# Weight quarters in two loads each, wider zero products, and another fixed order of the opening

## The chip, the cores and the metric

The kernel runs on one core of a Trainium2 chip. The metric is device time in microseconds (us): 188.25 us for the kernel before, the median of 4 runs from 188.14 to 188.42.

A core has five engines that run side by side: TensorE multiplies matrices (PE in the profile; its weight loads are PEld), VectorE (DVE), ScalarE (ACT) and GpSimd (POOL) work on tiles, and SyncE (SP) issues the transfers between the device memory and the core's own memory. Sixteen transfer engines carry these out.

## The reference

First a linear attention with decay, for 4 batches, 8 heads, 768 positions and a head width of 48. Then a feed-forward part on the 3072 rows of width 384 that come out.

```python
for t in range(S):
    cur = np.einsum('bhd,bhe->bhde', u[None] * kt, vt)
    y[:, :, t] = np.einsum('bhd,bhde->bhe', rt, state + cur)
    state = wt[:, :, :, None] * state + np.einsum('bhd,bhe->bhde', kt, vt)
...
x = np.ascontiguousarray(attn_out.transpose(0, 2, 1, 3)).reshape(B * S, H * D)
h = x @ w_in                      # 384 x 2048
g = np.maximum(0.01 * h, h)
out = (g @ w_out)                 # 2048 x 384
```

## The kernel before

**Tiles and stages.** The 3072 rows are 24 chunks of 128, six to a batch. Chunks 0 and 1, and 2 and 3, are handled as pairs (one load for both), the others singly. For a chunk, four loads bring w, k, r and v (lines 493). ScalarE takes the logarithm of w (tile lw, line 360), TensorE sums it along the positions (tiles cp, hp, op; lines 544, 554, 714), ScalarE takes exponentials (line 370), and products of these with r and k (tile rk, line 300) are transposed on TensorE (line 418; for chunks 12 and on by a transposing transfer, line 408) into rkT. Scores (lines 652, 764) are masked on VectorE (tile m, line 436), and with the state (s, sb) they give y (lines 669, 677, 794, 799; its last sum is line 467). y is transposed into xT (lines 481, 295, or by a transfer, line 473). The vector u is brought by a small load on ScalarE's queue and spread over the partitions by a product on TensorE (line 504).

**The feed-forward part.** Each of the two weight matrices is loaded in four quarters (lines 319 and 324), each as one transfer into a staging tile of the ring `in`, and cast to bf16 by two half casts on whichever engine the order says (lines 295, 297). For each chunk TensorE makes four groups of 12 products with w_in, one for each quarter (tile hp, line 837; "up"), ScalarE applies the activation (tile g, line 879), and four groups of 4 products with w_out (tile op, line 898; "down") give the output, which is copied and stored.

**What sets the order.** Every step is entered into a `Plan` with its engine, an assumed duration, its dependencies and a priority. `Plan.order` plays the steps forward in time, engine by engine, and the kernel emits the instructions in the order of the planned starts. The order of each engine is thereby fixed when the program is built. Steps named in the string `EARLY` (numbers count the steps in the order in which the code adds them; a letter picks the engine) get the highest priorities in the order of the string. The list `FIRST` gives the order in which the up and down groups of chunks 0 to 3 are entered. From chunk 4 on, ups of a chunk alternate with downs of the one before.

**Fillers.** Up to a planned time of 24 us (`WARM`), whenever the plan has TensorE waiting before a step, products with a tile of zeros are emitted (line 933); their result is not used.

```python
for _ in range(int((plan.start[i] - at) * 0.7 / 0.13)):
    nc.tensor.matmul(
        op_r.tiles[1][:, 0:256], lhsT=zeros[:, 0:128], rhs=zeros[:], start=True, stop=True)
at = plan.start[i] + plan.dur[i]
```

**The queue of loads.** SP issues the loads in this order: the first pair's w, k, r, v; the second's v, w, k, r; quarters 1 and 0 of w_in, quarter 0 of w_out, quarters 2 and 3 of w_in, quarters 1, 2 and 3 of w_out; then chunk 4's w and r, chunk 5's w, chunk 4's k and v, and so on.

Of the kernel before, what the change touches and what calls it, by code (L numbers as in the profile page):

```python
# [9 lines left out]
BF16 = mybir.dt.bfloat16  # L10
# [5 lines left out]
class Plan:  # L16
# [23 lines left out]
    def order(self):  # L40
        n = len(self.eng)
        users = [[] for _ in range(n)]
        left = [len(d) for d in self.deps]
        for i, d in enumerate(self.deps):
            for j in d:
                users[j].append(i)
        ready_at = [0.0] * n
        start, done = [None] * n, [0.0] * n
        free = {e: 0.8 for e in self.ENGINES}
        coming = {e: [] for e in self.ENGINES}  # L50
        ready = {e: [] for e in self.ENGINES}
        dma_free = 0.0
        flying = []
        for i in range(n):
            if not left[i]:
                heapq.heappush(coming[self.eng[i]], (0.0, i))
        events = [(0.8, e) for e in self.ENGINES]
        heapq.heapify(events)
        count = 0
        while events:  # L60
            now, e = heapq.heappop(events)
            if free[e] > now + 1e-9:
                continue
            while coming[e] and coming[e][0][0] <= now + 1e-9:
                _, i = heapq.heappop(coming[e])
                heapq.heappush(ready[e], (self.pri[i], i))
            if not ready[e]:
                if coming[e]:
                    heapq.heappush(events, (coming[e][0][0], e))
                continue  # L70
            _, i = heapq.heappop(ready[e])
            start[i] = now
            count += 1
            free[e] = now + self.dur[i] * (1.8 if e == "PE" and now < 6 else 1)
            if self.wire[i] is None:
                done[i] = free[e] + self.LAT[e]
            else:

                flying = [x for x in flying if x[0] > free[e]]
                while sum(x[1] for x in flying) + self.rows[i] > 3300:  # L80
                    free[e] = max(free[e], flying.pop(0)[0])
                dma_free = max(dma_free, free[e]) + self.wire[i]
                done[i] = dma_free + 1.7
                flying.append((done[i], self.rows[i]))
            heapq.heappush(events, (free[e], e))
            for j in users[i]:
                left[j] -= 1
                same = self.eng[j] == e and self.wire[i] is None
                ready_at[j] = max(ready_at[j], free[e] if same else done[i])
                if not left[j]:  # L90
                    f = self.eng[j]
                    heapq.heappush(coming[f], (ready_at[j], j))
                    heapq.heappush(events, (max(ready_at[j], free[f]), f))
        assert count == n, (count, n)
        self.start, self.done = start, done
        return sorted(range(n), key=lambda i: (start[i], i))
# [30 lines left out]
def kernel(  # L127
# [11 lines left out]
    nc = tc.nc  # L139
# [14 lines left out]
    AHEAD = 5  # L154

    PAIRS = (0, 2)
    PWIRE, WIRE = 1.53, 1.15
    WEIGHTS = [(4, 24.0)] * 8
    WARM = 24.0
    CASTS = 21  # L160

    EARLY = """
        0 4 1 2 3 5 8 61 7 6 12 58 11 16 13 14 15 21 32 59 17 23 24 18 20p 19 22 28 9a 60 29 30 10a 33
        25 26 31v 40 27 117 64 34 65a 51 36 41a 44 52 63 114 46 42 126 62 45 35 67 66 120 43 71 123 37
        53 47 129 68 132 48 69 135 72 38 75p 49 70 76 74 77p 78 50 81 79 73 87v 54 82 39 118a 85 80 96v
        83 119p 138 86 55 84a 91 115 116 56 95 88v 57 713 128p 715 89 714 97 717 716 127p 98v 719 718 99
        140 122p 729 90v 720 100 121 730 102 723 124a 125p 101 721 724 92v 103 722 727 93 130a 170 104
        94 725 728 131v 105 107 726 106v 731 108 133a 737 109 733 738 134v 110 734 747 136 137p 139 745
        111 748 141 735 142 112 746 144 154v 261 732 113 736 145 172 174 752 147 749 159 149p 155v 171
        146 739 753 148 742 750 200 156 158 152 143a 157v 150 160 755 229 153 151 176 743 162 161 177  # L170
        186 231 756 763 165 265 764 164 230 191 178 758 187v 740 765 232 179 163 759 751 181p 180 202
        233 166 188 766 204 167 190 182 173 245 184 767 206 168 185v 183a 754 192 169v 768 193 741 207
        769 246 194 209 201 771 208 234v 757 770 247 216 262 772 760 210
    """
    blocks = [1] * NCH

    FIRST = [(0,(0,1),(0,1,2,3)),(1,(0,1),(0,1)),(0,(2,),(0,)),(1,(0,1),(2,)),(0,(2,),(1,)),(1,(0,1),(3,)),(0,(2,),(2,3)),(0,(3,),(0,)),(1,(2,),(0,)),(0,(3,),(1,)),(1,(2,),(1,)),(0,(3,),(2,)),(1,(2,),(2,)),(0,(3,),(3,)),(1,(2,),(3,)),(1,(3,),(0,1,2,3))]
    assert sum(blocks) == NCH

    pool = ctx.enter_context(tc.tile_pool(name="pool", bufs=1))  # L180
# [8 lines left out]
    pmask = pool.tile([128, 2, 128], BF16, name="pmask")  # L189
    pev = pool.tile([128, 128], BF16, name="pev")  # L190
    pex = pool.tile([128, 128], BF16, name="pex")
    zeros = pool.tile([128, 256], BF16, name="zeros")
    halves = pool.tile([128, 2], BF16, name="halves")
    ident = pool.tile([128, 128], BF16, name="ident")
    ones = pool.tile([128, 1], BF16, name="ones")
# [34 lines left out]
    with tc.manual_schedule():  # L230
# [80 lines left out]
        win_s, wout_s = [], []  # L311
        JQ = NJ // NQ

        def weight_steps(q, which, pri):
            st = in_r.take()

            def load(st=st, q=q):
                if which == 0:
                    nc.sync.dma_start(
                        out=st.t[:].rearrange("p (t f) -> p t f", t=KT),  # L320
                        in_=w_in_v[:, :, q * 512 : (q + 1) * 512],
                    )
                else:
                    nc.sync.dma_start(
                        out=st.t[:].rearrange("p (t f) -> p t f", t=JQ),
                        in_=w_out_v[:, q * JQ : (q + 1) * JQ, :],
                    )

            ld = step("SP", 0.45, load, pri, writes=[st], wire=2.25, rows=(384, 512)[which])
            made = []  # L330
            for half in range(2):
                def cast(e, st=st, q=q, half=half):
                    if which == 0:
                        f0 = half * 256
                        o = w_in_b[:, :, q * 512 + f0 : q * 512 + f0 + 256]
                        i = st.t[:].rearrange("p (t f) -> p t f", t=KT)[:, :, f0 : f0 + 256]
                    else:
                        n = JQ // 2
                        o = w_out_b[:, q * JQ + half * n : q * JQ + (half + 1) * n, :]
                        i = st.t[:].rearrange("p (t f) -> p t f", t=JQ)[:, half * n : (half + 1) * n, :]  # L340
                    copy(e, o, i)

                made.append(step(
                    ("DVE", "ACT")[half], (0.8, 0.84)[half], cast, CASTS, reads=[st], deps=[ld],
                    DVE=0.8, ACT=0.84, POOL=1.2))
            (win_s if which == 0 else wout_s).append(made)

# [148 lines left out]
        def spread_u():  # L496
            u_row = step(
                "ACT", 0.5,
                lambda: nc.scalar.dma_start(out=ur[:], in_=u.rearrange("h d -> (h d)").unsqueeze(0)),
                -1, wire=0.05)  # L500
            up = pre_r.take()
            s_ub = step(
                "PE", 0.7,
                lambda: nc.tensor.matmul(up.t[:, 0:DM], lhsT=onef[:], rhs=ur[:], start=True, stop=True),
                -1, writes=[up], deps=[u_row])
            return step(
                "ACT", 0.5, lambda: nc.scalar.copy(out=ub[:], in_=up.t[:, 0:DM]), 0.05, reads=[up], deps=[s_ub])
# [411 lines left out]
        for n in range(NCH):  # L919
            if n >= LEAD:  # L920
                plan.deps[lns[n]].append(up_done[n - LEAD])
        for rank, word in enumerate(EARLY.split()):
            i = int(word.rstrip("avp"))
            plan.pri[i] = rank - 10000
            if word[-1] in "avp":
                plan.eng[i] = {"a": "ACT", "v": "DVE", "p": "POOL"}[word[-1]]
                plan.dur[i] = plan.alts[i][plan.eng[i]]

        at = 0.8
        for i in plan.order():  # L930
            if plan.eng[i] == "PE" and at < WARM:
                for _ in range(int((plan.start[i] - at) * 0.7 / 0.13)):
                    nc.tensor.matmul(  # L933
                        op_r.tiles[1][:, 0:256], lhsT=zeros[:, 0:128], rhs=zeros[:], start=True, stop=True)
                at = plan.start[i] + plan.dur[i]
            if plan.alts[i]:
                plan.fn[i](plan.eng[i])
            else:
# [31 lines left out]
```

## Time and profile before

| | |
|---|---|
| median of 4 runs | 188.25 us (188.14 to 188.42) |
| profiled execution | 188.15 us |
| its span, first to last instruction | 186.4 us |
| TensorE busy | 179.5 us, 2608 products |
| VectorE, ScalarE, GpSimd busy | 121.2, 115.9, 101.0 us |
| zero products | 60, 11.7 us of records |
| moved | 34.62 MB, mean 186 GB/s |

The profile is one execution. In a line of its timeline stand the start (us from the span's start), the duration, the engine, the line of the kernel, the operation, the tiles (out<-in), the shape and the count of instructions merged into it; square brackets give idle time before it and what ended it. Records of products overlap, since they are pipelined: from one to the next, the start counts. In the chain of waits a piece is a start, a duration and what the time went to; "issue" is time for which the profile shows no wait. Engines that are not the bottleneck may be idle at no cost.

### The profile page before, as it was taken

How to read it: one execution, taken by the hardware profiler on the slowest of the kernel's cores; microseconds unless marked ns; L12 is line 12 of the kernel's file. 1: busy time of each engine (PE TensorE's matmuls, PEld its weight loads, DVE VectorE, ACT ScalarE, POOL GpSimd, SP SyncE). 2: the span in 40 equal slices, each digit the busy share in tenths (PEclk: the TensorE clock that was granted, in tenths of full speed). 3: DMA queues.
4: the chain of work that ended last, by engine and by line, in shares of the span. 5: the costliest groups of instructions: out<-in, count | busy, mean ns of one | idle time of the engine just before them, and what ended most of it. 6: DMA issues, size and time to landing. Idle time of an engine off the chain costs nothing.

```text
span 186.4 us, 6316 instructions
## 1 busy us (share of the span) xinstructions
PE 179.5 (96%) x2608; PEld 140.5 (75%) x2608; DVE 121.2 (65%) x232; ACT 115.9 (62%) x254; POOL 101.0 (54%) x142
## 2 busy tenths in 40 slices
PE   7999998999999999999999999999999999999892
PEld 4576887877777788787878687778878778788671
DVE  2079994657777797887668786587556676725111
ACT  2395868488665887788677578645465554543330
POOL 7587961133975888878784474351784444620000
PEclk9999999999999999999999999999999999999999
DMA  6999999799498998797999797967999999481202
GB/s 148 261 262 371 387 373 309 151 183 209 121 236 180 210 195 180 167 196 170 176 213 177 169 195 142 219 134 164 219 137 221 173 211 148 102 125 42 67 0 84
DMA packets 116383, 34.62 MB, mean 186 GB/s; under 512 B 109697, under 2 KB 114818, under 8 KB 116354
## 3 DMA queue, kind: packets, MB, share of 16 engines
q1 hardware_dynamic: 116352, 34.22, 85.7%
q8 instruction: 20, 0.33, 0.7%
q14 instruction: 9, 0.07, 0.1%
q10 hardware_dynamic: 2, 0.00, 0.0%
HBM read 25.17 MB, written 4.72 MB: 160 GB/s over the span
## 4 chain that ended last, share of the span: by engine, by line
PE 89%; DVE 3%; DMA 2%; issue 2%; ACT 1%; POOL 1%
PE hp L837 34%; PE op L898 32%; PE op L933 3%; PE se L764 3%; DMA xT<-y 2%; PE yp L799 2%; PE cp L714 2%; PE yp L775 2%; PE yp L794 1%; PE so L418 1%; DVE m L436 1%; PE se L418 1%; POOL rk L300 1%; PE yp L481 1%; PE yp L677 1%
## 5 line engine op out<-in xcount | busy, mean ns | idle before, releaser
L879 ACT ACTIVATE g<-hp 128x512 bf16<-128x512 f32 x96 | 57.2, 597 | 41.0 <-PE hp L837 39.3
L837 PE MATMUL hp<-xT,w_in_b 128*128 128x128 bf16 x1152 | 78.0, 219 | 0.7 <-DMA xT<-y 0.7
L898 PE MATMUL op<-w_out_b,g 128*128 128x384 bf16 x384 | 75.2, 326 | 0.0
L837 PEld LDWEIGHTS <-w_in_b 128*128 128x128 bf16 x1152 | 68.5, 98 | 7.2 <-DMA xT<-y 1.1
L898 PEld LDWEIGHTS <-g 128*128 128x128 bf16 x384 | 33.5, 98 | 15.8
L300 POOL TENSOR_TENSOR sb<-s,a 128x384 bf16<-128x384 f32 x17 | 14.3, 843 | 29.2 <-DVE s L456 14.1
L300 POOL TENSOR_TENSOR ru<-in,ub 128x384 f32<-128x384 f32 x22 | 23.0, 1044 | 7.7 <-DMA in<-in_r_dram 7.7
L300 POOL TENSOR_TENSOR vs<-in,dg 128x384 f32<-128x384 f32 x22 | 18.9, 858 | 9.1 <-DVE dg L393 8.9
L436 DVE TENSOR_TENSOR m<-se,maskb 128x512 bf16<-128x512 f32 x20 | 13.7, 687 | 11.2 <-PE so L764 8.0
L300 POOL TENSOR_TENSOR ru<-ru,in 128x384 f32<-128x384 f32 x20 | 20.4, 1018 | 0.9
L467 DVE TENSOR_TENSOR y<-yp,vs 128x384 bf16<-128x384 f32 x24 | 13.3, 554 | 9.6 <-PE yp L799 6.6
L300 DVE TENSOR_TENSOR rk<-in,ek 128x384 bf16<-128x384 f32 x18 | 14.4, 798 | 3.7 <-ACT ek L370 3.7
L370 ACT ACTIVATE cp<-cp 128x384 f32<-128x384 f32 x22 | 10.6, 483 | 6.3 <-DVE ci L729 6.3
L729 DVE TENSOR_TENSOR ci<-cp,lw 128x384 f32<-128x384 f32 x20 | 11.0, 550 | 4.9 <-PE cp L719 3.3
L300 DVE TENSOR_TENSOR rk<-in,cp 128x384 bf16<-128x384 f32 x22 | 12.0, 547 | 3.2 <-ACT cp L370 2.6
L393 DVE TENSOR_REDUCE dg<-ru 128x8 f32<-128x384 f32 x24 | 13.0, 544 | 1.6 <-POOL ru L300 1.5
L360 ACT ACTIVATE lw<-in 128x384 bf16<-128x384 f32 x24 | 12.2, 521 | 2.9 <-DMA in<-in_w_dram 2.5
L436 DVE TENSOR_TENSOR m<-so,maskb 128x512 bf16<-128x512 f32 x20 | 13.6, 679 | 0.0
L297 DVE COPY o<-op 128x384 f32<-128x384 f32 x10 | 5.6, 555 | 11.7 <-PE op L898 11.5
L933 PE MATMUL op<-zeros 128*128 128x256 bf16 x60 | 11.7, 329 | 1.1 <-DVE zeros L268 1.1
L297 POOL CAST vb<-in 128x384 bf16<-128x384 f32 x19 | 10.5, 554 | 0.7 <-DMA in<-in_v_dram 0.7
L370 ACT ACTIVATE ek<-ci 128x384 f32<-128x384 f32 x20 | 10.4, 519 | 0.8 <-POOL ru L300 0.7
(117 smaller groups left out, 213.5 us busy)
## 6 DMA issues: line engine op xcount, KB each, us to landing
out_dram<-o SPq DMA_DIRECT2D x24, 192.0 KB, 3.0
in<-in_w_dram SPq DMA_DIRECT2D x20, 192.0 KB, 4.0
in<-in_r_dram SPq DMA_DIRECT2D x20, 192.0 KB, 3.7
in<-in_k_dram SPq DMA_DIRECT2D x20, 192.0 KB, 3.7
in<-in_v_dram SPq DMA_DIRECT2D x20, 192.0 KB, 3.7
in<-in_moe_w_in_dram SPq DMA_DIRECT2D x4, 768.0 KB, 11.4
in<-in_moe_w_out_dram SPq DMA_DIRECT2D x4, 768.0 KB, 13.1
in<-in_w_dram SPq DMA_DIRECT2D x2, 384.0 KB, 5.0
```

The source lines that it names most:

```text
L297: (nc.vector if e == "DVE" else nc.gpsimd).tensor_copy(out=o, in_=i)
L300: (nc.vector if e == "DVE" else nc.gpsimd).tensor_tensor(out=o, in0=a, in1=b, op=ALU.mult)
L360: lambda: nc.scalar.activation(out=lw.t[:, :, 0:D], in_=wn.t, func=AF.Ln),
L370: "ACT", 0.5, lambda: nc.scalar.activation(out=out.t[:], in_=i, func=AF.Exp, scale=scale),
L393: lambda: nc.vector.tensor_reduce(out=dg.t[:], in_=ru.t[:], axis=AX.X, op=ALU.add),
L436: lambda par=par: nc.vector.tensor_tensor(out=m.t[:, par], in0=gt(sc[par].t), in1=mask.unsqueeze(1).to_broadcast([128, NP, 128]), op=ALU.m ...
L467: lambda: nc.vector.tensor_tensor(out=y.t[:], in0=hd(yp.t[:, 0:DM]), in1=vs.t[:], op=ALU.add),
L729: lambda: nc.vector.tensor_tensor(out=ci.t[:], in0=hd(cp.t[:, 0:DM]), in1=lw.t[:, :, 0:D], op=ALU.add),
L837: nc.tensor.matmul(hp.t[:, a * N : (a + 1) * N], lhsT=w_in_b[:, t, (j + a) * 128 : (j + a + 1) * 128], rhs=xT[:, t, c0 : c0 + N], start=(a ...
L879: lambda hp=hp, g=g, j=j, J=J, N=N: nc.scalar.activation(out=g.t[:, j : j + J, 0:N], in_=hp.t[:, 0 : J * N].rearrange("p (a n) -> p a n", ...
L898: nc.tensor.matmul(op.t[:, 0:DM], lhsT=g.t[:, j, off : off + 128], rhs=w_out_b[:, j, :], start=(j == 0), stop=(j == NJ - 1))
L933: nc.tensor.matmul(op_r.tiles[1][:, 0:256], lhsT=zeros[:, 0:128], rhs=zeros[:], start=True, stop=True)
```

## The change

- Each weight quarter is loaded by two transfers instead of one, each of half the bytes, into halves of the same staging tile. A half of w_in has runs of 1024 bytes (2048 before), a half of w_out has runs of 768 bytes (1536 before). Each half cast waits for its own load. For w_out the halves are now split along the columns.
- The zero products are 512 columns wide, with at most one of 256 behind them, and their number follows from the planned wait divided by 0.44; the planner assumes TensorE to be slow until 8 us (6 before), and the u load and its product are entered as longer.
- Steps of `EARLY` on one engine now also depend on one another in the order of the string; the string is new and longer (383 steps, 272 before), and so is `FIRST`.

In the new order SP issues the first pair's w, r, k, v; the second's k and w; the second half of quarter 1 of w_in; the second pair's v and r; both halves of quarter 0, the other half of quarter 1, quarters 2 and 3; then w_out's quarters 1 and 0 (as 1, 0, 0, 1), chunk 4's w, w_out's quarters 2 and 3, and chunk 4's r, k, chunk 5's w, chunk 4's v.

TensorE's order around the first groups, before and after (up and down with chunk and quarter, `T` a transpose of rk, `yt` of y, `sc` scores, `st` state):

```
before: ... y1, T3, T3, yt1, st2, up 0.0, up 1.0, up 0.1, up 1.1, down 0.0, sc2, down 1.0, up 1.2, up 0.2,
        y2, up 1.3, up 0.3, yt2, sc3, down 0.1, up 2.1, ...
after:  ... T2, y1, T3, T2, yt1, up 0.0, T3, up 1.0, up 0.1, st2, up 1.1, up 0.2, up 1.2, sc2, up 0.3, up 1.3,
        y2, sc3, down 0.0, yt2, down 1.0, down 1.1, up 2.0, ...
```

```diff
-            free[e] = now + self.dur[i] * (1.8 if e == "PE" and now < 6 else 1)
+            free[e] = now + self.dur[i] * (1.8 if e == "PE" and now < 8 else 1)
...
-    PWIRE, WIRE = 1.53, 1.15
+    PWIRE, WIRE, WWIRE = 1.53, 1.15, (1.12, 1.12)
...
     EARLY = """
-        0 4 1 2 3 5 8 61 7 6 12 58 11 16 13 14 15 21 32 59 17 23 24 18 20p 19 22 28 9a 60 29 30 10a 33
...
+        0 4 2 1 3 5 8 59 7 6 13 58 32 36v 12 17 11 16 22 33 120 14 21 30 15 37 20 24 31 61 23 26 25a 9
...
-    FIRST = [(0,(0,1),(0,1,2,3)),(1,(0,1),(0,1)),(0,(2,),(0,)),(1,(0,1),(2,)),(0,(2,),(1,)),...
+    FIRST = [(0,(0,1),(0,1,2,3)),(0,(2,3),(0,)),(1,(0,1),(0,)),(0,(2,3),(1,)),(1,(0,1),(1,)),...
...
-    zeros = pool.tile([128, 256], BF16, name="zeros")
+    zeros = pool.tile([128, 512], BF16, name="zeros")
...
-            ld = step("SP", 0.45, load, pri, writes=[st], wire=2.25, rows=(384, 512)[which])
...
+                part = st.t[:, half * 768 : (half + 1) * 768].rearrange("p (t f) -> p t f", t=(KT, JQ)[which])
+                if which == 0:
+                    f0 = q * 512 + half * 256
+                    src, dst = w_in_v[:, :, f0 : f0 + 256], w_in_b[:, :, f0 : f0 + 256]
+                else:
+                    n0 = half * DM // 2
+                    src = w_out_v[:, q * JQ : (q + 1) * JQ, n0 : n0 + DM // 2]
+                    dst = w_out_b[:, q * JQ : (q + 1) * JQ, n0 : n0 + DM // 2]
+                ld = step(
+                    "SP", 0.45, lambda part=part, src=src: nc.sync.dma_start(out=part, in_=src), pri,
+                    writes=[st], wire=WWIRE[which], rows=(384, 512)[which])
...
-                -1, wire=0.05)
+                -1, wire=0.75)
...
-                "PE", 0.7,
+                "PE", 1.6 / 1.8,
...
+            if plan.wire[i] is None:
+                plan.deps[i] += behind.get(plan.eng[i], [])
+                behind[plan.eng[i]] = [i]
...
-                for _ in range(int((plan.start[i] - at) * 0.7 / 0.13)):
+                wait = plan.start[i] - at
+                for n in [512] * int(wait / 0.44) + [256] * int(wait % 0.44 / 0.22):
                     nc.tensor.matmul(
-                        op_r.tiles[1][:, 0:256], lhsT=zeros[:, 0:128], rhs=zeros[:], start=True, stop=True)
-                at = plan.start[i] + plan.dur[i]
+                        op_r.tiles[1][:, 0:n], lhsT=zeros[:, 0:128], rhs=zeros[:, 0:n], start=True, stop=True)
+                at = plan.start[i] + plan.dur[i] * (1.8 if plan.start[i] < 8 else 1)
```

## The prediction

> **What bounds the kernel now.** I read the page's part 1 first, then TensorE's timeline of the first 34 us, the chain of waits, the transfer rates by stretch, and the chain's end.
>
> ```profile
> PE 179.5 (96%) x2608; PEld 140.5 (75%) x2608; DVE 121.2 (65%) x232; ACT 115.9 (62%) x254; POOL 101.0 (54%) x142
> ...
> L933 PE MATMUL op<-zeros 128*128 128x256 bf16 x60 | 11.7, 329 | 1.1 <-DVE zeros L268 1.1
> ```
>
> TensorE carries the span, but 60 of its products multiply zeros. All but one lie before the first product of the feed-forward part (w_in, line 837):
>
> ```profile
> 1.12 2.74 PE L933 MATMUL op<-zeros 128*128 128x256 bf16 x12 [1.12 <-DVE zeros L268]
> 3.79 1.64 PE L504 MATMUL op<-ur,onef 1*128 1x384 f32 x2
> 5.37 2.31 PE L933 MATMUL op<-zeros 128*128 128x256 bf16 x10
> 7.48 0.85 PE L544 MATMUL hp<-lw,pev 128*128 128x384 bf16 x2
> ...
> 22.38 1.50 PE L837 MATMUL hp<-xT,w_in_b 128*128 128x128 bf16 x24
> ```
>
> The feed-forward part starts at 22.4. ScalarE's timeline says why: its cast of the needed weight half ran from 21.64 to 22.49. That weight had landed at 20.4 (issue 11.7, 8.7 to landing).
>
> The chain of waits then shows one hole, and after it TensorE is full for 142 us:
>
> ```profile
> 31.04 0.14 PE se L652
> 31.22 0.84 issue
> 32.05 0.21 PE se L652
> 32.28 0.02 PE se L652
> ```
>
> "issue" means that nothing in the profile was waited for. The page's instruction queue moved only 20 packets, 0.33 MB (about 16 KB each). At 31.0 TensorE had just reached a step of 64 tiny instructions (32 products with their weight loads), so I read the hole as late instructions.
>
> The transfers are the other limit of the opening; columns end with clock, transfer share, GB/s:
>
> ```profile
> 6.00:12.00 6.00, 5.78 (x50) 3.92 (x49) 2.39 (x6) 2.90 (x8) 3.46 (x10) 1.00 1.28 261
> 16.00:30.00 14.00, 13.54 (x289) 11.26 (x290) 12.95 (x23) 10.62 (x20) 9.91 (x11) 1.00 1.06 379
> ```
>
> Pair loads (runs of 384 bytes) move at 261 GB/s and land 1.5 us apart, at 4.5, 6.0 ... 15.0. Weight quarters (2048 and 1536 bytes, 786 KB) move at 379 and land 2.05 us apart, at 20.4 to 33.0. The queue never empties.
>
> At the end the last chunk's output is just late:
>
> ```profile
> 171.66 3.93 DMA xT<-y
> 175.60 0.05 issue
> 175.64 1.51 PE hp L837 x24
> ```
>
> TensorE idles 0.72 us here. The profiled execution took 188.15 us: span 186.4 plus 1.75 around it; the median of four is 188.25, 0.10 more. My sum is made against 188.15.
>
> **The change, part by part.**
>
> *Opening fillers.* The planner fills a planned wait with zeros. For the same numbers as the code of before uses (12 and 10 products, as the trace shows), the new rule gives, by hand, 6 wide and 1 narrow before the product for u (planned wait 3.75 - 0.8 = 2.95) and 2 wide before the first sums (wait 1.06). A narrow one takes 2.74/12 = 0.228, so a wide one 0.43 to 0.46 at that clock. The decays (lw) were ready at 4.55 + 0.94 = 5.49, yet the sums started at 7.48, behind ten zeros. Now: u ends near 5.65, two wide fillers end at 6.5. Gain 1.0 us for chunk 0's chain, bounds 0.5 to 1.9. It isn't on the final path by itself, since the weights decide next; without it the next term would lose up to 1 us.
>
> *Half loads and their place.* I counted the steps in the order the code adds them, so that the new order can be read. One half (of quarter 1) goes ahead of the second pair's v and r; then come both halves of quarter 0. One half at 379 GB/s is 393 KB/379 = 1.03 us. Landings: the pair's last load at 15.0 + 1.03 = 16.05. In the trace the first two weights came 5.4 after the last pair load, 1.3 more than their 4.1; I keep the 1.3: quarter 0 at 18.4 and 19.4, then 20.4, 21.5, 22.5, 23.5, 24.6, and the second matrix 25.6, 26.6, 27.7, 28.7.
>
> *The chain to the first product.* Sums at 6.5 take 0.64, 0.64 and 0.9 (rows of before: 7.48 to 8.12, 8.33 to 9.2), so the last exponentials end near 9.65; VectorE's four products, one now 0.84 long and taken over from GpSimd, end at 10.5, a transpose and ScalarE's copy (0.58) at 11.6, scores at 12.0 (13.3 before). Then VectorE in its new order, start to start: four masks 2.4, state 0.5, sum 0.5, y 0.5, a product 0.8, copy 0.35, two products 1.0, y 0.55, which ends y of chunk 1 at 18.6 and its transpose at 18.9; the delayed r (16.05) is needed at 17.1. So not the attention but the cast decides: 19.4 + 0.85 = 20.25, against 22.38. From there TensorE's new order, with start-to-start times of the trace (0.67 a group of 12, 0.65 a down group, 0.43 and 0.4 for state and scores, 0.9 for y): two groups with a transpose to 22.65, state 23.1, 23.75, two groups of quarter 2 (cast ready 23.4) to 25.1, scores 25.5, two of quarter 3 (25.45) to 26.85, y 27.75, scores 28.15, first down (27.7 + 0.65) to 29.05, transpose, second down to 29.95. The same work is done in the old trace at 32.46. Gain 2.5 us: 1.5 from the earlier start (2.13 less a transpose and a state step moved behind it, 0.23 + 0.43), 0.84 from the hole, 0.2 of fillers between the groups.
>
> *Twice as many issues.* Eight more loads on SP's queue, each 0.45 to 1.5 of issue; behind them wait chunk 4's loads. Hidden: SP already waited up to 5.2 us on one issue, because transfers were the limit. Were the cover gone, 8 x 0.55 = 4.4 us at chunk 4's loads, which have some 4 us of slack (last landing 37.4, 6.6 of chain, needed at 47.5). I take 0.
>
> *Shorter runs.* No row has 1024 or 768 bytes. Between the nearest rows (23.4 ns a packet and engine for 384 bytes at 261 GB/s, 65.5 for 1536) a straight line gives 46.8 and 37.4 ns: 1.12 and 1.20 us a half. Eleven halves precede the first down: 8 x 0.09 + 3 x 0.17 = 1.2 us lost. The other end is the full rate, 0. The 192-byte loads reach no more per byte than the 384-byte ones, and 1536 no less than 2048, so the rows look like two rates rather than a cost per packet; I take 0.2. The Trainium skill (DMA: Bandwidth & Descriptors, Specifications) puts the line rate at 512 bytes and over, which would make this term 0. The same page (Bandwidth) asks for transfers of 1 MiB for 75% of peak, and its fit of 2.0 us plus bytes at 436 GB/s would price each half at an estimated 2.9 us, 46 us for 16 of them end to end; the 384-KB pair loads that land 1.5 us apart speak against it, and by that price the kernel would be far slower.
>
> *Fewer fillers when warm.* About 0.49 of each planned wait against 0.59. A 256-wide product took 0.23 until 8.1 and 0.13 from 9.4; useful work alone fills some 8.4 of the 13.7 us between 6.5 and 20.25 (the attention steps of two pairs, by the durations above). I take 0. If the clock fell back, the bound is 8.4 us more work time, of which half lies in waits: 4 us.
>
> *Instructions.* Some 45 fillers fewer, each with a weight load, shift the fetches; a step of 80 tiny instructions soon after the next scores may still wait. Bounds 0 to 0.8; I take 0.3.
>
> *The rest.* From 30 to 47.5 (sum of the order's groups) TensorE has work at hand; chunk 4's y then has to come 2.4 us earlier than before, within its slack. The end: order after the listed steps is planned anew. Bounds: the 0.72 goes, or grows as below. I take 0.
>
> Sum: -2.5 + 0.2 + 0.3 = -2.0 us: 188.15 - 2.0 = 186.15, or 186.2 on the median.
>
> **The rivals.**
>
> *The gain is given back at the end.* The last chunk's r landed at 159.3, and 16 us of chain (transposing transfer 5.0, masks, y, transfer 3.9) led to 175.64. Transfers run at a share of 1.16 from 140 to 160. If these loads don't move, the 0.72 hole becomes 2.7 and the time is 188.15; with new interleavings 187.9 to 188.6. Against it: SP's queue there mostly waits for engines (6.5 us for TensorE's groups, 5.3 for VectorE's products), which move up together.
>
> *Slower: the halves arrive late.* If short runs fall to the pair loads' 261 GB/s, a half costs 1.50. The first down moves 11 x 0.47 = 5.2 us, and the loss is 5.2 - 2.5 = 2.7: 190.8. It decides at 1.03 + 2.5/11 = 1.26 us a half (312 GB/s). For it: the shorter runs in the trace are at the low rate. Against: both longer ones are at the high one. Smaller forms, with a stalled fixed order behind one late half, reach 189.2.
>
> *No effect:* part of the first rival; the listed order surely changes what TensorE does.
>
> **How the numbers follow.** Forecast 0.66, given back 0.15, late halves 0.19. A measurement here can tell about 0.2% (0.38 us). Faster by more than that: the forecast and a little of the second, 0.68; same 0.10; slower 0.22. Low end: all of 2.5 and the 0.72, 188.15 - 3.2 = 184.95, with the median's 0.1, 185.0. The high end takes in the given-back case and the smaller late-half cases: 189.2. What lies above (late halves in full) and below leaves out under 2 in 10. The likeliest case alone: 185.0 to 187.7.
>
> **What would show it.** Right: first sums near 6.5, first L837 near 20.3, weights landing about 1.03 us apart to 33, no hole over 0.5 us near 31, TensorE full from 30, a last hole under 1 us. Wrong: halves over 1.2 us apart; a hole of more than 2 us before the last chunk's L837; 256-wide zeros at 0.23 after 10 us; new holes called "issue".

## The result and the profile after

The changed kernel takes 186.87 us, the median of 38 executions (186.14 to 188.46); the kernel before takes 188.15 us in 59 executions beside them (186.25 to 188.84). The ratio is 0.9948, 95% interval 0.9933 to 0.9963: faster by half a per cent. The forecast was 186.2 us (185.0 to 189.2). The executions of both kernels spread over 2 us, so a ratio says more here than one time. Single executions far slower than the others of their kernel (295.32 us of before, 353.83 of b_halves, 599.84 of b_nowarm, and the profiled one of a_oldzeros, 190.71) are left out of the ratios.

The profiled execution of the changed kernel took 187.38 us, span 185.7 (before: 188.15 and 186.4), 0.77 us less. The page, part 1, and the group of the zero products in the groups by line (busy, mean ns of one, idle before):

```profile
PE 177.1 (95%) x2572; PEld 136.3 (73%) x2572; DVE 122.2 (66%) x232; ACT 116.9 (63%) x253; POOL 103.6 (56%) x143
L932 PE MATMUL op<-zeros 128*128 128x512 bf16 (+1 forms) x24 | 8.4, 439 | 1.3 <-DVE zeros L273 1.3
```

24 zero products where there were 60. Now TensorE's timeline of the opening:

```profile
1.25 2.95 PE L932 MATMUL op<-zeros 128*128 128x512 bf16 x7 [1.25 <-DVE zeros L273]
...
6.54 0.85 PE L538 MATMUL hp<-lw,pex 128*128 128x384 bf16 x2
...
20.08 0.38 PE L412 MATMUL so<-ident,rk 128*128 128x128 bf16 x4 [1.31 <-ACT rkT L300]
...
20.80 0.83 PE L831 MATMUL hp<-xT,w_in_b 128*128 128x128 bf16 x12
...
29.68 0.82 PE L892 MATMUL op<-w_out_b,g 128*128 128x384 bf16 x4 [0.19 <-ACT g L873]
30.35 0.33 PE L475 MATMUL yp<-ident,y 128*128 128x128 bf16 x3
30.51 1.46 PE L892 MATMUL op<-w_out_b,g 128*128 128x384 bf16 x8
```

The first sums start at 6.54 (7.48 before), the first up at 20.80 (22.38), and the hole in the scores near 31 is gone. The third down group starts at 31.16 (two groups of the last line lie together, 0.65 apart), against 32.39 in the trace of before. TensorE has done the same work by then, so 1.23 us are won at this point. The line with 1.31 is an idle gap behind ScalarE: its copy of rkT is queued behind the cast that waits for the first half of quarter 0.

The rate of the transfers, in the same stretch as in the prediction (last columns clock, transfer share, GB/s):

```profile
16.00:30.00 14.00, 11.86 (x282) 9.93 (x281) 10.68 (x19) 9.79 (x19) 10.12 (x11) 1.00 1.09 329
```

329 GB/s in place of 379 (chunk 4's w, in runs of 192 bytes, is a small part of this stretch): short runs cost about what the straight line of the prediction said. And the chain of waits has two new pieces. One is the r of chunk 4:

```profile
31.18 6.44 DMA in<-in_r_dram
37.63 0.03 issue
37.65 0.02 DVEq L305
37.67 0.04 issue
37.72 0.57 DVE rk L305
38.28 0.05 issue
38.33 0.40 PE se L412 x4
```

A load issued at 31.18 lands at 37.6, VectorE makes rk, and TensorE's next transposes can only start at 38.33, 0.46 us after the products ahead of them were through. In before that r landed at 34.1. So the first up of chunk 4 starts at 49.13 against 49.90: 0.77 us are left of 1.23. The other piece is near the end:

```profile
163.70 5.12 DMA rkT<-rk
168.86 0.23 PE se L758
```

The transposing transfer of the last chunk's rk holds its scores back; TensorE loses 0.95 us from 167.9 on. It loses nothing at the last chunk's up groups, where before lost 0.72 by the idle column (0.88 from product to product). One end hole takes the place of the other, and TensorE's last product ends at 182.28 against 183.05: again 0.77 less, which is the whole difference of the two profiled executions.

### The profile page after: what moved, and what is told of

The parts are those of the page before. It is cut to its first block, busy times and chain, and to the rows that moved or that the text cites. A ratio compares the mean times of both kernels' runs of the same rounds, so it can differ in the third digit from the quotient of the medians.

```text
span 185.7 us, 6238 instructions
## 1 busy us (share of the span) xinstructions
PE 177.1 (95%) x2572; PEld 136.3 (73%) x2572; DVE 122.2 (66%) x232; ACT 116.9 (63%) x253; POOL 103.6 (56%) x143
## 4 chain that ended last, share of the span: by engine, by line
PE 75%; DMA 11%; SPq 11%; issue 1%; DVE 1%; POOL 0%; DVEq 0%
PE op L892 31%; PE hp L831 30%; SPq L334 6%; DMA in<-in_moe_w_in_dram 5%; SPq L487 5%; DMA in<-in_r_dram 3%; PE se L758 3%; DMA rkT<-rk 3%; PE yp L793 2%; PE cp L708 2%; PE yp L769 2%; PE yp L788 2%; PE se L412 1%; PE so L412 1%; PE yp L475 1%
## 5 line engine op out<-in xcount | busy, mean ns | idle before, releaser
L305 POOL TENSOR_TENSOR ru<-in,ub 128x384 f32<-128x384 f32 x22 | 23.5, 1066 | 17.3 <-DMA in<-in_r_dram 15.4
L305 POOL TENSOR_TENSOR ru<-ru,in 128x384 f32<-128x384 f32 x22 | 22.9, 1043 | 1.3
L305 POOL TENSOR_TENSOR sb<-s,a 128x384 bf16<-128x384 f32 x14 | 12.8, 912 | 18.4 <-DVE s L450 14.3
L305 DVE TENSOR_TENSOR rk<-in,ek 128x384 bf16<-128x384 f32 x17 | 13.2, 774 | 0.4 <-ACT ek L364 0.3
L302 POOL CAST vb<-in 128x384 bf16<-128x384 f32 x20 | 11.0, 551 | 3.9 <-DMA in<-in_v_dram 3.5
L450 DVE TENSOR_TENSOR s<-yp,sb 128x384 f32<-128x384 f32 x14 | 7.7, 553 | 3.6 <-PE yp L769 3.2
```

The lines of the kernel that those rows point to most:

```text
L302: (nc.vector if e == "DVE" else nc.gpsimd).tensor_copy(out=o, in_=i)
L305: (nc.vector if e == "DVE" else nc.gpsimd).tensor_tensor(out=o, in0=a, in1=b, op=ALU.mult)
```

## The experiments

The times of the opening are read from the traces as above: start of the first sums, of the first up group, of the third down group, and of chunk 4's first up, then the end of TensorE's last product. "Holes" are from product to product, beyond the usual distance. Each row is one profiled execution (the ratio is from all of the label's executions against before). a_oldzeros has no row, as its profiled execution ran at a granted clock of 0.95.

| kernel | sums | first up | third down | chunk 4 up | end | zeros | ratio |
|---|---|---|---|---|---|---|---|
| before | 7.48 | 22.38 | 32.39 | 49.90 | 183.05 | 60 | 1 |
| after | 6.54 | 20.80 | 31.16 | 49.13 | 182.28 | 24 | 0.9948 |
| b_zeros | 6.32 | 21.82 | 30.80 | 48.58 | 180.90 | 27 | 0.9879 |
| b_halves | 7.47 | 22.64 | 31.83 | 49.33 | 182.67 | 60 | 1.0013 |
| b_split256 | 6.33 | 21.83 | 31.93 | 49.44 | 181.70 | 45 | 0.9937 |
| b_nowarm | 6.33 | 21.82 | 32.23 | 49.73 | 181.99 | 10 | 0.9918 |
| b_swap | 6.33 | 19.86 | 31.01 | 48.50 | 180.65 | 27 | 0.9899 |
| a_outrows | 5.51 | 20.68 | 30.74 | 48.38 | 180.66 | 24 | 0.9886 |
| a_longruns | 6.54 | 20.56 | 30.40 | 48.34 | 181.42 | 24 | 0.9914 |
| a_longruns_512 | 6.33 | 20.91 | 31.41 | 49.40 | 182.20 | 16 | 0.9904 |

Names with b_ start from the kernel before, with a_ from the changed one. Two accounts were to be told apart. In mine the shorter runs cost the changed kernel what is missing from the forecast; in the other the new order or the instruction fetches do.

**a_outrows: w_out's halves by rows, so that their runs are 1536 bytes again.**

```diff
-                    n0 = half * DM // 2
-                    src = w_out_v[:, q * JQ : (q + 1) * JQ, n0 : n0 + DM // 2]
-                    dst = w_out_b[:, q * JQ : (q + 1) * JQ, n0 : n0 + DM // 2]
+                    j0 = q * JQ + half * JQ // 2
+                    src, dst = w_out_v[:, j0 : j0 + JQ // 2, :], w_out_b[:, j0 : j0 + JQ // 2, :]
```

> The changed kernel, but the halves of w_out are cut along the rows, so that their runs stay 1536 bytes (768 in the change); w_in keeps its halves of 1024. Theory (the gain was cut down by the short runs): a w_out half goes from 1.20 us back to 1.05, quarter 0 is complete 3 x 0.15 = 0.45 us earlier, the first down group (29.68) starts near 29.2, chunk 4's r lands 1.2 us earlier and the 0.30 us hole at 38 is gone; about 0.7 us faster than the changed kernel, ratio to the kernel before 0.991 (0.989 to 0.994). Rival (the run length hides behind other work): same as the changed kernel, 0.995, first down at 29.7.

Measured: 186.01 us (185.73 to 186.16), ratio 0.9886 (0.9848 to 0.9924), below the changed kernel's interval, and a little more than was expected. The first down moves from 29.68 to 29.26, the r of chunk 4 lands at 35.2 instead of 37.6, and the transposes behind it no longer wait (TensorE's timeline):

```profile
36.95 0.81 PE L891 MATMUL op<-w_out_b,g 128*128 128x384 bf16 x4
37.59 0.39 PE L411 MATMUL se<-ident,rk 128*128 128x128 bf16 x4
```

Chunk 4's ups start 0.75 us earlier (0.57 against the second profile of the changed kernel, after_again). Order, fillers and the number of loads are the same, so the 768-byte runs alone cost the changed kernel 0.6 to 0.75 us by then: 0.35 to 0.42 in the weights and the rest in chunk 4's wait. The end hole, too, shrinks from 0.95 to 0.18, as the last rkT transfer is issued at 162.45 instead of 163.70; why by more than the 0.75 isn't shown.

**b_zeros: the kernel before, with the new zero products alone.**

```diff
-                for _ in range(int((plan.start[i] - at) * 0.7 / 0.13)):
+                wait = plan.start[i] - at
+                for n in [512] * int(wait / 0.44) + [256] * int(wait % 0.44 / 0.22):
...
-                at = plan.start[i] + plan.dur[i]
+                at = plan.start[i] + plan.dur[i] * (1.8 if plan.start[i] < 8 else 1)
```

> The kernel before with only the zero products of the change (512 wide, counted by the planned wait over 0.44, the slow clock counted in). Theory: the first sums start near 6.5 instead of 7.5, the first up group stays at 22.4 since a weight cast sets it, and with some 70 instructions fewer the fetch no longer falls into the scores at 31, so the 0.84 us hole there shrinks or moves: 0.2 to 0.9 us faster, ratio 0.995 to 0.999. Rival (the hole at 31 has another cause, fillers only fill): hole of 0.8 at 31 stays, ratio 1.000.

Measured: 185.92 us (185.72 to 186.10), ratio 0.9879 (0.9837 to 0.9920), more than twice the gain that was expected at most. This small part of the change is worth more than the whole of it. The sums start 1.16 us earlier, the first up 0.56; the hole in the scores is gone, as is the hole at the end. The order and the loads are those of before, and the third down group is at 30.80, earlier than in the changed kernel. A smaller stop is left in the up groups behind it (TensorE's timeline):

```profile
31.45 1.73 PE L837 MATMUL hp<-xT,w_in_b 128*128 128x128 bf16 x23
```

Elsewhere 24 such products take 1.50 us; here one starts 0.33 us after the one before it, where 0.06 is usual. The profiles add up: 0.56 at the first up, 1.03 (from start to start) for the hole, 0.27 given back here and 0.88 at the end make 2.20, and TensorE's last product ends 2.15 us earlier.

**a_oldzeros: the changed kernel with the old zero products (the last diff reversed).**

> The changed kernel with the old zero products (256 wide, 0.7/0.13 of the wait, no slow clock). Theory: the first sums start about 1 us later (7.5), but the first up group still waits for its weight and starts within 0.3 us of 20.8; more instructions shift the fetches and may bring a hole of up to 0.8 us; ratio to the kernel before 0.995 to 0.999. Rival (the fillers bring the gain): first up group at 21.8 or later and the gain gone, ratio 1.000 or more.

Measured: 187.87 us, ratio 1.0001 (0.9967 to 1.0035). The new order and the half loads give nothing without the new fillers. The profiled execution ran at a granted clock of 0.95 throughout, so its times are not compared with the others, and I read the place of its stall; the size at full clock isn't shown. In TensorE's timeline the scores stop in the middle:

```profile
31.56 0.21 PE L646 MATMUL se<-rkT 48*64 48x64 bf16 x1 [2.15 <-issue]
```

2.15 us for which nothing in the profile was waited for, the same thing as the 0.84 us of before, at another size.

**b_halves: the kernel before with half loads alone (split as in the change, both halves issued where the quarter was, in the old order).**

```diff
-                    nc.sync.dma_start(
-                        out=st.t[:].rearrange("p (t f) -> p t f", t=KT),
-                        in_=w_in_v[:, :, q * 512 : (q + 1) * 512],
-                    )
...
+            def load():
+                for half in range(2):
+                    part, src, _ = views(half)
+                    nc.sync.dma_start(out=part, in_=src)
```

> The kernel before, in its own order, with only the loads cut in two as in the change (1024 and 768 bytes), both halves issued one after the other. Theory (halves cost transfer time, the order brings the gain): the eight quarters take 8 x 1.12 + 8 x 1.20 = 18.6 us instead of 16.5, the last lands near 35 instead of 33, the first up group stays at 22.4, and the kernel is 0.3 to 1.5 us slower, ratio 1.002 to 1.008. Rival (the halves with their earlier casts bring the gain): first up group earlier than 22.0 and ratio 0.995 to 0.998.

Measured: 188.39 us, ratio 1.0013 (0.9982 to 1.0045): no difference that can be told. The rate is close to that of the changed kernel, although its order is the old one (transfers by stretch):

```profile
16.00:30.00 14.00, 13.45 (x288) 11.10 (x286) 13.36 (x23) 10.50 (x20) 9.50 (x11) 1.00 1.10 339
```

The last weight lands at 34.96 instead of 33.04. That the third down group still starts 0.56 us earlier comes from the hole in the scores, 0.14 us here: the products were later than in before, the instructions came when they came. A loss on the weights was covered by a smaller stall.

**b_split256: b_zeros, each 512-wide product as two of 256.** The same time in fillers with 36 more instructions of TensorE.

```diff
-                for n in [512] * int(wait / 0.44) + [256] * int(wait % 0.44 / 0.22):
+                for n in [256] * (2 * int(wait / 0.44)) + [256] * int(wait % 0.44 / 0.22):
```

> The kernel before with the new count of zero products, but each 512-wide one given as two of 256: the same filler time, 36 TensorE instructions more than with the wide ones (30 fewer than before). Theory (an instruction fetch that comes too early in the work leaves TensorE dry in the scores of chunk 3): the first sums stay at 6.3 and the first up group at 21.8, but a hole of 0.3 to 0.9 us called issue is back in the scores near 30.6; ratio to the kernel before 0.990 to 0.994. Rival (the shorter opening, not the instruction count, brought the gain of the wide zeros): no hole and 0.988 as with the wide ones.

Measured: 186.81 us (ratio 0.9937, 0.9910 to 0.9965); its fastest execution (186.24) is slower than the slowest of b_zeros (186.10). The opening is the same to 0.01 us up to the first down; then the hole in the scores is back:

```profile
31.72 0.21 PE L652 MATMUL so<-rkT 48*64 48x64 bf16 x1 [0.91 <-issue]
```

So most of the gain at 31 us in b_zeros does not come from the time that the fillers take, but from their number.

The transfer records show the way. The instruction queue moves 20 packets of 16 KB; TensorE has 5216 instructions in before (2608 products, as many weight loads), so a packet is some 256 of them. Counted in the traces, the place of the stop is the same in every kernel that has it: TensorE has started 479 weight loads and 479 products, and the next weight load comes 2.4 to 2.9 us after the start of the third packet.

| kernel | third packet starts | product 479 starts | TensorE goes on | stop, start to start |
|---|---|---|---|---|
| before | 29.51 | 31.02 | 32.05 | 1.03 |
| b_split256 | 29.12 | 30.62 | 31.72 | 1.10 |
| b_halves | 29.09 | 31.28 | 31.49 | 0.21 |
| b_zeros | 29.36 | 31.57 | 31.89 | 0.33 |
| a_oldzeros (clock 0.95) | 28.71 | 29.22 | 31.56 | 2.34 |
| a_outrows | 29.28 | 31.67 | 31.87 | 0.20 |
| a_longruns | 29.12 | 31.33 | 31.82 | 0.49 |
| a_longruns_512 | 30.96 | 32.89 | 33.41 | 0.52 |
| after | 28.87 | 32.09 | 32.15 | none |

What stands at this place differs: scores in before, b_halves, b_split256 and a_oldzeros, an up group in b_zeros, a_outrows, a_longruns and after, a small sum of lw in a_longruns_512. Fillers ahead of it are counted too, so fewer of them put later work there. The stop is long where TensorE gets there soon after the packet's start; the changed kernel gets there 3.2 us after it, and nothing stops (after_again, b_nowarm and b_swap, 2.7 to 3.4 us after it, do not stop either). That the packets are TensorE's is read from these counts and times. The Trainium skill (Runtime: NRT & Kernel Launch, Instruction fetch mechanics) says that an engine's instructions come in blocks of 16 KiB, 256 instructions, which agrees with these counts, and that the fetch is mostly hidden. Here it isn't: 0.84, 0.91 and 2.15 us.

**b_nowarm: b_zeros with fillers up to 8 us only.** 17 zero products fewer.

```diff
-            if plan.eng[i] == "PE" and at < WARM:
+            if plan.eng[i] == "PE" and at < 8:
```

> The kernel before with the new zero products only up to 8 us of the plan; none after. 34 instructions fewer still. Theory: the useful products alone keep the clock, the 384-wide sums near 13 us take 0.16 each, the first up group stays at 21.8 and no hole comes in the scores at 30.5; ratio 0.985 to 0.990. Rival (fillers keep the clock up): sums at 13 us take 0.32 each, the first up group comes 0.5 us or more later, ratio 0.992 or more.

Measured: 187.11 us, ratio 0.9918 (0.9886 to 0.9950). Three of the executions are at 187.1, two at 185.9 and 186.1. The busy times by stretch of the profiled one (187.10; the column before the last two is the granted clock):

```profile
12.00:18.00 6.00, 3.44 (x101) 2.67 (x86) 5.79 (x11) 3.87 (x11) 4.55 (x6) 1.00 1.14 332
18.00:20.00 2.00, 1.74 (x42) 1.42 (x40) 2.00 (x4) 1.82 (x4) 2.00 (x3) 0.60 1.07 381
20.00:22.00 2.00, 1.44 (x21) 1.03 (x22) 1.55 (x3) 1.63 (x3) 1.21 (x2) 0.50 1.06 384
22.00:24.00 2.00, 2.00 (x21) 2.00 (x20) 1.83 (x5) 0.60 (x1) 1.39 (x2) 0.50 1.05 386
24.00:26.00 2.00, 2.00 (x28) 2.00 (x26) 2.00 (x3) 0.95 (x2) 1.64 (x2) 0.69 1.06 378
```

TensorE is busy for 3.44 of 6 us from 12 to 18, with no gap over 1.1 us, and then works at half clock from 18 to 25. The third down group comes 1.43 us later than in b_zeros. The fillers after 8 us do keep the clock, and useful products alone do not.

**a_longruns: a_outrows with quarters 2 and 3 of w_in loaded whole (2048-byte runs).**

```diff
+                if which == 0 and q >= 2:
+                    part = st.t[:].rearrange("p (t f) -> p t f", t=KT)[:, :, half * 256 : (half + 1) * 256]
...
+                    elif half == 1:
+                        nc.sync.dma_start(
+                            out=st.t[:].rearrange("p (t f) -> p t f", t=KT),
+                            in_=w_in_v[:, :, q * 512 : (q + 1) * 512])
```

> The changed kernel with w_out halves cut along the rows (1536 bytes) and quarters 2 and 3 of w_in loaded whole (2048 bytes); order unchanged. Theory (run length sets the arrival): quarter 0 of w_out complete 0.4 us earlier than with the row halves alone, first down group near 28.9, ratio to the kernel before 0.985 to 0.988. Rival (arrival no longer decides): as with the row halves alone, 0.989, first down at 29.3.

Measured: 186.30 us (185.57 to 187.69), ratio 0.9914 (0.9880 to 0.9948): no better than a_outrows, as the rival had it, although the first down starts at 28.92, as the theory had it. The third down group is 0.34 us earlier (30.40), but chunk 4's ups start at 48.34 against 48.38. Between them lies a gap of 0.43 us at 31.3 (0.27 by the idle column), put down to "issue":

```profile
31.82 0.51 PE L841 MATMUL hp<-xT,w_in_b 128*128 128x128 bf16 x6 [0.27 <-issue]
```

What the weights gave, a fetch took. Two of the six executions, 187.19 and 187.69 us, have a granted clock of 0.991.

**a_longruns_512: a_longruns without the narrow zero products.** 8 products, 16 instructions fewer.

```diff
-                for n in [512] * int(wait / 0.44) + [256] * int(wait % 0.44 / 0.22):
+                for n in [512] * int(wait / 0.44):
```

> The kernel after with w_out's halves by rows and w_in's quarters 2 and 3 whole (as a_longruns), and without the 256-wide zero products: 16 TensorE instructions fewer before 24 us. My theory: the 0.43 us of issue at 31.3 us in a_longruns stands where an instruction packet came late for a dense step; with 16 instructions fewer the packet boundary lies elsewhere, so that this gap changes (gone, or under 0.2 us, if the boundary leaves the dense step), and the ratio goes from 0.991 to between 0.984 and 0.989. Rival: the gap has nothing to do with the count of instructions and stays at 0.4 us, ratio 0.989 to 0.993; or the granted clock falls below 1.00 before 26 us for want of the narrow fillers, and the ratio is above 0.993.

Measured: 185.86 us (185.49 to 187.73), ratio 0.9904 (0.9865 to 0.9942), not told apart from a_longruns. Both expectations have their part. Eight of ten executions are between 185.49 and 185.91. The profiled one (187.36) is one of the two others, and its clock fell; the busy times by stretch:

```profile
20.00:22.00 2.00, 2.00 (x22) 2.00 (x20) 1.52 (x3) 1.44 (x3) 0.77 (x1) 0.50 1.07 388
```

In its trace the gap has left the up group and stands eight products further on in the program, 0.45 us long:

```profile
33.41 0.23 PE L723 MATMUL cp<-ones,lw 128*128 128x1 bf16 x3 [0.35 <-issue]
```

It is again behind 479 weight loads: with 16 instructions fewer ahead the gap moves by as many in the program, as the theory said. It got no shorter in this execution, whose clock had fallen; how long it is at full clock isn't shown.

**b_swap: b_zeros with quarter 0 of w_in loaded before quarter 1.**

```diff
+            if which == 0:
+                q = (1, 0, 2, 3)[q]
...
-                m1.append((up, j, J, N, g, chs, [xt_steps[ch] for ch in chs] + win_s[j * 128 // 512]))
+                m1.append((up, j, J, N, g, chs, [xt_steps[ch] for ch in chs] + win_s[(1, 0, 2, 3)[j * 128 // 512]]))
```

> The kernel before with only the new zero products, and quarters 0 and 1 of w_in in each other's place: quarter 0 is loaded first and its half casts take the places of quarter 1's; the products keep their order. My theory: there the first up group waited for the cast of quarter 0, which landed second (first up at 21.82 us, VectorE's cast just before). With quarter 0 first, its cast is early, and the first group starts when xT is ready, near 20.9 us; the groups of quarter 1 follow after two groups (1.4 us), when its cast is done. Some 0.5 to 0.9 us come off the start; the ratio goes from 0.988 to between 0.983 and 0.987. Rival: TensorE's work between 21 and 31 us only moves its gap, the second quarter's cast is late instead, and the ratio stays at 0.988 within 0.002.

Measured: 185.74 us (185.53 to 185.98), ratio 0.9899 (0.9866 to 0.9932). The median is 0.18 us under that of b_zeros, so the rival holds. The first up starts 1.96 us earlier than in b_zeros, over twice what my theory said; yet TensorE's timeline shows where it goes:

```profile
19.86 0.94 PE L839 MATMUL hp<-xT,w_in_b 128*128 128x128 bf16 x12
...
24.67 0.81 PE L900 MATMUL op<-w_out_b,g 128*128 128x384 bf16 x4
```

The first down is at 24.67, in b_zeros at 24.68: one late up group is replaced by later gaps and zeros. An early first up was worth nothing by itself here; what counted is where TensorE first stays full, about 31 us.

**after_again: the changed kernel, profiled once more.**

> The changed kernel once more, for another profile. Theory (the last hole comes when a 16-KB instruction packet shares a transfer engine with the last chunk's transposing transfer): if such a packet lies inside the transfer of rkT or xT, TensorE waits 0.7 to 1.0 us before the last chunk and the time is 187.2 to 187.6; if not, there is no hole and 186.1 to 186.8. Rival (the hole belongs to the order): the hole of 0.95 at 168 is there whatever the packets do.

Measured: 187.14 us, span 185.4. Every start up to the third down group agrees within 0.1 us (6.54, 20.75, 31.08), chunk 4's wait is 0.36 us, and the hole at the last chunk's scores is there again, at 0.60 us. So these belong to the kernel, not to one execution. An instruction packet (165.91, 1.65 us long) lies inside the transfer of rkT this time as well, so theory and rival are not told apart, and the hole is shorter than the 0.7 to 1.0 us of the theory; in a_outrows one of 1.24 us lies inside, and the hole is 0.18.

## Why the prediction was right, and where it was not

**Opening fillers.** Sums forecast at 6.5, measured 6.54. That it isn't on the final path was said of this kernel, and the runs agree: in b_zeros the same step brought the first up only 0.56 us, and in a_outrows, whose execution had the sums a whole microsecond earlier still (5.51), the first up moved by 0.12.

**First up.** Forecast 20.25, measured 20.80: the halves landed at 18.69 and 19.81 instead of 18.4 and 19.4, and ScalarE's cast began 0.12 us after landing. The mechanism, cast and not attention, was right: ScalarE's cast ends at 20.76.

**Shorter runs: the failed term.** The prediction had a straight line with 1.12 and 1.20 us a half, and took 0.2 us instead of the 1.2 that it gives. The trace has six gaps between landings of w_in from 18.69 to 25.43, 1.12 each, and three of w_out to 29.05, 1.21 each. The straight line was exact. By the landings (393 KB each) 1024-byte runs move at 351 GB/s and 768-byte runs at 325, between 261 for 384 bytes and 379 for 1536 and 2048: a cost per packet, not two rates. The reason that was given for two rates, the 192-byte loads, speaks against them: the trace of before moves 192-byte runs at 197 GB/s (36 to 38 us, transfer share 1.02), 15.6 ns a packet, where the prediction's own line gives 16.4. The Trainium skill (DMA: Bandwidth & Descriptors, Specifications) puts the line rate at 512 bytes and over; these numbers contradict it. With the right size, the third of w_out's halves lands at 29.05 and not 27.7, and the first down starts at 29.68 and not 28.4. With it the sum would have read -2.5 + 1.2 = -1.3 at the third down group, where -1.23 was measured. The runs bear the size out: 1536-byte runs for w_out (a_outrows) bring that group 0.42 us earlier, and whole quarters 2 and 3 of w_in on top (a_longruns) 0.34 more, where the line gives 0.51 and 0.36.

**Twice as many issues, hidden by slack.** Wrong in its slack. The 4 us (3.5 by the numbers given with them) were counted to chunk 4's first up, but in TensorE's fixed order chunk 4's transposes stand near 37.9, and its r, issued seven us later than in before, came too late for them: 0.46 us. a_outrows shows that the runs, and not the number of issues alone, made it too late: it has as many issues, its r lands at 35.2, and nothing waits.

**Instructions.** Taken as 0.3 us of loss for the changed kernel; the hole was gone. But the sum credited its 0.84 us to the new order. The runs show the new order with the old fillers stalling in the scores (a_oldzeros, 2.15 us in an execution at clock 0.95), and the old order with the new fillers not (b_zeros, 0.33 us from start to start in a later up group). It was the number of instructions ahead, and when TensorE gets there: the prediction reckoned with some 45 fillers fewer (36 were) but worked out neither, so that the changed kernel does not stop at all is luck.

**Fewer fillers when warm.** The size, 0, was right for the profiled execution of the changed kernel, with the clock at 1.00 throughout; the reason, that useful products alone keep it, was wrong. Nor does it hold in every execution: eight of the changed kernel's have a mean granted clock of 0.991 or less and a median of 187.4 us, the others 186.7; of before, no listed execution but that of 295.32 us is under 0.997. a_oldzeros with its 55 zero products has such executions too, and b_zeros with 27 has none, so the number of fillers alone does not explain them; what does stays open. The price of losing it in b_nowarm was 1.2 us by the medians of b_nowarm and b_zeros, below the bound of 4; two of five executions paid little or nothing.

**The end.** Taken as 0; it was 0, as the sum of 0.88 won at one hole and 0.95 lost at another. That these cancel is luck. Before's hole at the last up groups did not come from late work alone: in before and b_halves, an instruction packet of 1.5 to 1.6 us falls into the last transposing transfer of y, which lands 3.9 to 4.0 us after its issue there; in the nine other profiles at full or nearly full clock no packet lies inside, and it lands after 2.3. In a_oldzeros (clock 0.95), with a packet of 1.0 us inside, it takes 3.1. That the packet delays the transfer fits all of these, but no run here moved the packet alone. What sets the issue of the last rkT, and so the 0.95, stays open.

**The rivals.** Halves came 1.12 to 1.21 us apart, short of the 1.26 at which the loss was to begin, though 1.21 is just over the 1.2 that was named as a sign of being wrong. Of the first rival, a hole before the last chunk came (0.95 us), but at another place and not over 2 us. What came true is the forecast with about half of its size: -0.77 by the profiles, -1.28 by the medians, where -2.0 was forecast.

The sum of the whole: -2.5 as forecast, +1.2 for the runs (0.2 taken), +0.46 at chunk 4, 0 at the end make -0.84, and -0.77 was measured. Four kernels have medians from 185.7 to 186.0 us (b_swap, a_longruns_512, b_zeros, a_outrows), by different ways, and the intervals of b_zeros, a_outrows and b_swap lie wholly under that of the changed kernel. The plainest is one part of the change by itself: the kernel before with wider zeros, at 185.92.

## What to carry to other kernels

A change of several parts is priced part by part, and each part is tried alone: here three lines of fillers are worth 1.2%, and the large rest of the change takes some of it back. Where two known rates bracket an unknown run length, price the transfer by the straight line of time per packet, and count a load's slack to the first step that waits for it in a fixed order, not to the step that seems to matter. When a tight sequence of small instructions shows idle time called "issue", count the instructions ahead of it: here the stall stayed at one count, and taking some out, or putting some in, changed what stood there and how early TensorE came to it.

## What the runs showed of the hardware

Three things I had not expected. A TensorE that is 57% busy for 6 us, with gaps of at most 1.1 us, lost half of its clock for some 7 us. The Trainium skill (TensorE: Matmul & The Clock Gate, What's actually happening) has the clock fall after an idle window of some 3.4 us, and no gap here is near that; the same page (A second HAM failure mode: psum-queue depth-cycling) tells of a clock that falls with frequent short idling, which fits b_nowarm. Instructions reach TensorE in packets of 16 KB, and with the weights streaming eight traces show 2.4 to 2.9 us from a packet's start until the engine goes on, always at the same count of instructions. And time per packet of a load on one transfer engine rises in a line with its length: 192 bytes 16 ns, 384 bytes 24, 768 bytes 38, 1024 bytes 47, 1536 bytes 65 (each an estimate, 16 times the length over the rate above).
